# A decode-attention kernel on Trainium2: PV's matmuls from a nested hardware loop instead of straight code

## The chip, the cores and the metric

The kernel runs on one core of one Trainium2 chip. The metric is the device time of one execution in microseconds (us); smaller is better. Every time below is a median of fast runs, unless a single run is named. A profile's span is about 2 us shorter than the run's time.

## The reference, cut to what matters

One token (x of 640) goes through layer norm, then through attention over a cache of 32 heads, 32768 positions and 128 values per position, and in parallel through a small gated MLP. Both are added to x.

```python
q = (xn @ wq) per head                                   # 640 -> 32 x 128
scores = einsum("bhqd,bhkd->bhqk", q, k) * (128 ** -0.5) # k: [1, 32, 32768, 128] bf16
p = softmax(scores)
o = einsum("bhqk,bhkd->bhqd", p, v)                      # "PV"
out = x + o @ wo + (silu(xn @ w_gate) * (xn @ w_up)) @ w_down
```

K and V are 8.4 MB per head each. The weights are small beside them.

## The kernel before

In this kernel each engine has its own program, and they wait for each other at semaphores. Three slots of SBUF (`ring`) hold K or V of one head. VectorE multiplies K by q in place, in four quarters of 4.4 us. TensorE sums groups of products by identity matmuls into PSUM, and VectorE reduces them to scores. ScalarE takes the exponential. TensorE then does PV: 64 matmuls per head, each with its own four columns of P as the stationary operand and 512 columns of V streaming, all accumulated into one PSUM tile `O`. The PV of head h-1 comes after the scores of head h.

The heads 2 to 31 run in a hardware loop of three heads per pass (`t.Fori`). Inside it, PV was written out:

```python
PARTS = [64, 64, 128]      # PV of a head in three parts; W = 4 columns per matmul
def pv_part(h, part):
    s = slot_of[("v", h)]
    if part == 0:
        wait(s_exp, ...); wait(s_o4, ...); wait(s_slot[s], ...)   # P is there, O is free, V has landed
    first = sum(PARTS[:part])
    for j in range(first, first + PARTS[part], W):
        mm = t.matmul(O, lhsT=P[:, h % PR, j:j + W], rhs=ring[:, s, j * DH:(j + W) * DH],
                      start=(j == 0), stop=(j + W == NJ))
    if part == len(PARTS) - 1:
        mm.then_inc(s_pv, 1)

def head(h):
    scores(h)
    if h >= 1: total(h - 1); pv_part(h - 1, 0)   # total: sum of the exponentials, one small matmul
    turn(h)                                       # maximum of the scores, transposed
    if h >= 1: pv_part(h - 1, 1)
    spread(h)                                     # maximum to all partitions
    if h >= 1: pv_part(h - 1, 2)
    if h >= 2: fold(h - 2)                        # four rows of O to one column
# ... [cut: the loop over heads]
pv_last(0); total(H - 1); fold(H - 2)             # the last head's V comes in two halves
pv_last(1); hidden_part(0); fold(H - 1); hidden_part(1)
# ... [cut: out projection and down projection, small matmuls to the end]
```

The DMA queue is issued by SyncE. The next V waits for the end of a head's scores, and the next K for the end of a PV, because these free the slots.

Of the kernel before, what the change touches and what calls it, by code (L numbers as in the profile page):

```python
# [8 lines left out]
BF16 = mybir.dt.bfloat16  # L9
# [3 lines left out]
def bass_parallel_sum__gqa_block_cached__swiglu_ffn__decode_kernel(  # L13
# [15 lines left out]
    DH = A_k_cache.shape[3]  # L29
# [3 lines left out]
    NJ = SK // 128  # L33
# [4 lines left out]
    CE = NJ * DH  # L38
# [6 lines left out]
    PR = 3  # L45
    SR = 3
    TAIL = [NJ // 2, NJ // 2]
    RB = DH // 32
    OC = H * DH // 128
    WTAIL = [8, 8, 8, 5, 2, 1]  # L50
    PARTS = [64, 64, 128]
    W = 512 // DH
    assert sum(PARTS) == NJ and NHF == 4 and (H - H0) % PER == 0 and PER % SLOTS == 0
    assert PER % PR == 0 and PER % SR == 0
    assert OC == 32 and H * RB == 128 and sum(WTAIL) == OC
    HA = 5
# [13 lines left out]
    for pos, u in enumerate(units):  # L70
        s = pos % SLOTS
# [6 lines left out]
    with ExitStack() as es:  # L78
        def sbt(name, shape, dtype):
            return es.enter_context(nc.sbuf_tensor(name, shape, dtype))  # L80

        def sem(name):
            return es.enter_context(nc.semaphore(name))

        ring = sbt("ring", [128, SLOTS, CE], BF16)
        qb = sbt("qb", [128, H * DH], BF16)
        sc = sbt("sc", [128, NJ], F32)
        P = sbt("P", [128, PR, NJ], BF16)
# [4 lines left out]
        ocol = sbt("ocol", [128, H], BF16)  # L93
        oblk = sbt("oblk", [128, H, RB], BF16)
        blk = sbt("blk", [128, RB], BF16)
        fold32 = sbt("fold32", [128, OC], BF16)
        ot = sbt("ot", [128, OC], BF16)
        hcol = sbt("hcol", [128, FB + 1], BF16)
        par = sbt("par", [128, 2], F32)
        sg = sbt("sg", [128, 2, FB], F32)  # L100
        one1 = sbt("one1", [1, 1], BF16)
        xf = sbt("xf", [128, NCD], F32)
# [18 lines left out]
        s_const = sem("const")  # L121
# [7 lines left out]
        s_exp, s_pv, s_o4, s_fold, s_ov = sem("exp"), sem("pv"), sem("o4"), sem("fold"), sem("ov")  # L129
# [5 lines left out]
        flat = ring[:, :, :].rearrange("p s n -> p (s n)")  # L135
# [32 lines left out]
        u0 = d0 + FM * D + D // 2  # L168
        g0 = WO_S * CE + OC * D
        FW = FB * 128  # L170
# [24 lines left out]
        def relay(copy, i, c):  # L195
            w = (wg_v, wu_v)[i][:, c, :]
            if (i, c) in rest:
                return copy(rest[i, c].rearrange("p (f t) -> p f t", t=2),
                            w[:, FM * 128:F][:, :, None].to_broadcast([128, FL, 2]))
            copy(even(i, c)[:, 0:FM * 128].rearrange("p (j m) -> p j m", j=FM),  # L200
                 w[:, 0:FM * 128].rearrange("p (m j) -> p j m", j=FM))
            return copy(even(i, c)[:, FM * 128:FW].rearrange("p (f t) -> p f t", t=2),
                        w[:, FM * 128:F][:, :, None].to_broadcast([128, FL, 2]))
        wo = flat[:, WO_S * CE:WO_S * CE + OC * D]
        wo_v = wo.rearrange("p (j c m) -> p j c m", j=OC, c=NCD)
        assert OC * D <= CE
# [23 lines left out]
        with nc.psum_tensor("ps8", [128, 8, 512], F32) as ps8:  # L230
            bank = [ps8[:, b, :] for b in range(8)]
            O = ps8[0:W, 4, :]
            OL = ps8[0:W, 5, :]
# [44 lines left out]
            @block.gpsimd  # L278
            def pool(g):
                n = [0]  # L280

                def done(ins):
                    ins.then_inc(s_const, 1)
                    n[0] += 1
                    g.wait_ge(s_const, n[0])

                for t in (ident, identf):
                    done(g.memset(t[:, :], 0.0))
                    done(g.affine_select(out=t[:, :], in_=t[:, :], compare_op=ALU.not_equal, fill=1.0, base=0,
                                         pattern=[[-1, 128]], channel_multiplier=1))  # L290
                done(g.memset(blk[:, :], 0.0))
                for a in range(RB):
                    done(g.tensor_copy(out=fold32[a * 32:(a + 1) * 32, :],
                                       in_=ident[a * 32:(a + 1) * 32, a * 32:a * 32 + OC]))
                for a in range(RB):
                    done(g.memset(blk[a * 32:(a + 1) * 32, a:a + 1], 1.0))
                assert n[0] == 5 + 2 * RB
                g.wait_ge(s_out, 16)

            @block.tensor  # L300
            def pe(t):
# [3 lines left out]
                for c in range(NCD):  # L305
                    mm = t.matmul(misc[:, 8 + c:9 + c], lhsT=xrow_v[:, :, c], rhs=one1[:, :], start=True, stop=True)
                for c in range(NCD):
                    mm = t.matmul(misc[:, 16 + c:17 + c], lhsT=xrow[:, c * 128:(c + 1) * 128], rhs=one1[:, :],
                                  start=True, stop=True)
# [9 lines left out]
                for b in range(NQB):  # L319
                    for c in range(NCD):  # L320
                        mm = t.matmul(bank[b], lhsT=xnb[:, c, :], rhs=wq_v[:, c, b * 512:(b + 1) * 512],  # L321
                                      start=(c == 0), stop=(c == NCD - 1))
                    mm.then_inc(s_q, 1)
                t.wait_ge(s_qc, NQB)
                t.wait_ge(s_const, 4)

                def again(out, lhsT, rhs, stop):

# [9 lines left out]
                def scores(h):  # L338
                    kv = ring[:, slot_of[("k", h)], :].rearrange("p (j d) -> p j d", d=DH)
                    for i in range(NHF):  # L340
# [9 lines left out]
                                mm = again(ob, ident[:, :], src, g == DH // G - 1)  # L350
                        mm.then_inc(s_qk, 1)

                def pv_part(h, part):
                    s = slot_of[("v", h)]
                    if part == 0:
                        wait(s_exp, h, lambda h: h + 1)
                        wait(s_o4, h, lambda h: h)
                        wait(s_slot[s], h, lambda h: 16 * use_of[("v", h)])
                    first = sum(PARTS[:part])
                    for j in range(first, first + PARTS[part], W):  # L360
                        mm = t.matmul(O, lhsT=P[:, h % PR, j:j + W], rhs=ring[:, s, j * DH:(j + W) * DH],  # L361
                                      start=(j == 0), stop=(j + W == NJ))
                    if part == len(PARTS) - 1:
                        mm.then_inc(s_pv, 1)

                def pv_last(i):
                    h = H - 1
                    s = slot_of[("v", h)]
                    if i == 0:
                        t.wait_ge(s_exp, h + 1)  # L370
                    t.wait_ge(s_tail[i], 16)
                    first = sum(TAIL[:i])
                    for j in range(first, first + TAIL[i], W):
                        mm = t.matmul(OL, lhsT=P[:, h % PR, j:j + W], rhs=ring[:, s, j * DH:(j + W) * DH],  # L374
                                      start=(j == 0), stop=(j + W == NJ))
                    return mm

                def fold(h):

# [26 lines left out]
                def head(h):  # L406
                    scores(h)
                    if h >= 1:
                        total(h - 1)
                        pv_part(h - 1, 0)  # L410
                    turn(h)
                    if h >= 1:
                        pv_part(h - 1, 1)
                    spread(h)
                    if h >= 1:
                        pv_part(h - 1, 2)
                    if h >= 2:
                        fold(h - 2)


                def hidden_part(i):
                    for n, c in enumerate(ORDER[i]):
                        if (i, c) in A_COPIES:
                            t.wait_ge(s_even[0], A_COPIES.index((i, c)) + 1)
                        else:
                            t.wait_ge(s_even[1], v_copies.index((i, c)) + 1)
                        for j in range(FB):
                            mm = t.matmul(ffn[:, i * FB + j:i * FB + j + 1],
                                          lhsT=hidden(i, c, j), rhs=xn[:, c:c + 1],
                                          start=(i == 0 and n == 0 and j == 0),  # L430
                                          stop=(i == 1 and n == NCD - 1 and j == FB - 1), skip_group_check=True)
                    return mm
# [27 lines left out]
                with t.Fori(0, (H - H0) // PER) as i:  # L460
                    group[0] = i
                    for h in range(H0, H0 + PER):
                        head(h)
                    group[0] = None
                pv_last(0)
                total(H - 1)
                fold(H - 2)
                pv_last(1).then_inc(s_pv, 1)
                hidden_part(0)
                fold(H - 1)  # L470
                hidden_part(1).then_inc(s_f, 1)
                t.wait_ge(s_const, 5 + 2 * RB)
                t.wait_ge(s_ob, 1)
                t.matmul(op, lhsT=oblk[:, :, :], rhs=fold32[:, :], start=True, stop=True).then_inc(s_op, 1)
                t.wait_ge(s_ot, 1)
# [72 lines left out]
            def dve(v):  # L548
# [78 lines left out]
                for n, (i, c) in enumerate(v_copies):  # L627
                    if n == 0 or v_copies[n - 1][0] != i:
                        v.wait_ge(s_ffn[i], 16)
                    relay(lambda out, in_: v.tensor_copy(out=out, in_=in_), i, c).then_inc(s_even[1], 1)  # L630
                v.wait_ge(s_const, 5 + 2 * RB)
                v.tensor_reduce(out=par[:, :], in_=ident[:, :].rearrange("p (f t) -> p t f", t=2),
                                axis=AX.X, op=ALU.add).then_inc(s_fd, 1)
                v.wait_ge(s_ov, H + 1)
# [49 lines left out]
```

## Time and profile before

| | before |
|---|---|
| time | 1288.1 us |
| bytes read | 554 MB, 431 GB/s over the span |
| period of one head in the loop | 38.70 us (K and V, 19.35 us each) |
| PV, first to last start | 14.21 us per head |

Two lines of the page of before: busy us and share of the span of each engine, then the busy share of the DMA engines in tenths, over 40 slices of the span:

```profile
PE 1042.9 (81%) x4971; PEld 256.8 (20%) x3051; DVE 683.7 (53%) x417; ACT 62.9 (5%) x147; POOL 2.5 (0%) x17
...
DMA  9999999999999999999999999999999999999998
```

Transfers fill every slice. TensorE looks nearly as busy (81%), but it is not the limit, as the timeline shows. Its columns are start in us, duration in us, engine, line, operation, and in brackets the idle time of the engine before it with what ended it. One head of before:

```profile
596.73 17.43 DVE L595 TENSOR_TENSOR ring<-ring,qb 128x8192 bf16<-128x8192 bf16 x4 [9.67 <-DMA ring<-in_A_k_cache_dram]
...
617.88 0.33 SPq L260 DMA_DIRECT2D ring<-in_A_v_cache_dram  x1
...
617.89 3.62 PE L361 MATMUL ps<-ring,P 128*4 128x512 bf16 x16
...
625.41 7.07 PE L361 MATMUL ps<-ring,P 128*4 128x512 bf16 x32
...
632.41 1.05 PE L383 MATMUL ps<-identf,o 4*128 4x1 f32 x8
632.51 0.33 SPq L251 DMA_DIRECT2D ring<-in_A_k_cache_dram  x1
...
639.91 0.61 PE L348 MATMUL ps<-ring,ident 128*128 128x512 bf16 x1 [6.45 <-DVE ring L595]
```

K lands and VectorE starts at 596.73. The scores end at 617.88, which issues the next V. PV follows in three parts (16, 16 and 32 matmuls; the second, of 3.62 us, is left out here), and its end at 632.41 issues the next K. After the fold TensorE is idle for 6.45 us until the first quarter of the next head is multiplied.

The trace also keeps sequencer instructions, those that set registers or branch. Here are two of the outer loop's edge, a fused instruction of three register operations and the branch back (count, then minimum, median and maximum ns; the columns after that are first and last start):

```profile
L460 PEldq FUSED_REGOPS  x10: 50/50/50, 90.6 to 1133.6; - x10
...
L460 PEldq COMPARE_BRANCH  x10: 76/208/235, 204.6 to 1249.5; - x10
```

The tail of before, TensorE alone, from the last part of PV(30) to the last small matmuls of the projections:

```profile
1244.62 7.07 PE L361 MATMUL ps<-ring,P 128*4 128x512 bf16 x32
...
1252.60 7.07 PE L374 MATMUL ps<-ring,P 128*4 128x512 bf16 x32
...
1260.89 7.07 PE L374 MATMUL ps<-ring,P 128*4 128x512 bf16 x32
...
1267.89 1.65 PE L428 MATMUL ps<-xn,ring 128*128 128x1 bf16 x41
...
1270.19 1.05 PE L383 MATMUL ps<-identf,o 4*128 4x1 f32 x8
...
1278.31 2.52 PE L454 MATMUL ps<-ot,ring 128*128 128x1 bf16 x80
...
1281.56 0.58 PE L454 MATMUL ps<-ot,ring 128*128 128x1 bf16 x16 [0.74 <-DMA ring<-in_A_wo_dram]
1282.92 0.78 PE L454 MATMUL ps<-ot,ring 128*128 128x1 bf16 x24 [0.78 <-issue]
```

TensorE works almost without pause from 1244 us. It waits only at the end: for pieces of wo and for causes that the profile calls "issue" (nothing that it shows). These waits and the 0.38 us at 1277.27 (not shown) add up to 1.9 us of idle time. Counted from the start of one matmul to the start of the next, which leaves out the modelled ends, the pauses at 1277.27, 1279.60, 1281.56 and 1282.92 delay the chain by 2.5 us.

### The profile page before, as it was taken

The numbers are of one execution on the slowest core, as the hardware profiler recorded it, in microseconds if no ns is written. First come the engines' busy times: TensorE is split into PE (matmuls) and PEld (weight loads), VectorE is DVE, ScalarE is ACT, GpSimd is POOL, SyncE is SP. The second block draws the span as 40 slices with busy tenths as digits, with TensorE's granted clock in tenths as the row PEclk, the third lists the DMA queues.
The fourth block names the chain that finished last, engine by engine and source line by source line (L and its number), as shares of the span: only waits on it lengthen the run. The fifth ranks groups of instructions, "written<-read, shape, count | busy, mean of one in ns | idle before, by whom it ended". The sixth has DMA issues, their size and how long they took to land.

```text
span 1285.9 us, 9499 instructions
## 1 busy us (share of the span) xinstructions
PE 1042.9 (81%) x4971; PEld 256.8 (20%) x3051; DVE 683.7 (53%) x417; ACT 62.9 (5%) x147; POOL 2.5 (0%) x17
## 2 busy tenths in 40 slices
PE   3599777789777788777798777788777798778798
PEld 1011112221112221112221112221112221112225
DVE  0855665445665445664446664446664446654444
ACT  2000000000000000000000000000000000000003
POOL 0000000000000000000000000000000000000000
PEclk9799888898888999888898888898888998888898
DMA  9999999999999999999999999999999999999998
GB/s 422 427 444 431 429 434 437 430 430 442 428 434 432 436 430 434 438 428 434 434 436 428 436 438 426 434 436 434 434 430 438 428 432 442 428 434 432 436 418 357
DMA packets 10965, 554.13 MB, mean 431 GB/s; under 512 B 1227, under 2 KB 1484, under 8 KB 1740
## 3 DMA queue, kind: packets, MB, share of 16 engines
q1 hardware_dynamic: 10954, 554.00, 99.7%
q8 instruction: 7, 0.11, 0.0%
q14 instruction: 2, 0.02, 0.0%
q10 hardware_dynamic: 2, 0.00, 0.0%
HBM read 553.99 MB, written 0.00 MB: 431 GB/s over the span
## 4 chain that ended last, share of the span: by engine, by line
DMA 53%; PE 27%; DVE 13%; issue 7%; DVEq 0%; SPq 0%
DMA ring<-in_A_k_cache_dram 51%; PE ps L361 17%; DVE ring L595 13%; PE ps L329 8%; DMA ring<-in_A_wo_dram 2%; PE ps L348 1%; PE ps L403 0%; PE ps L397 0%; PE ps L391 0%; PE ps L454 0%; SPq L273 0%; DVEq L595 0%; DVE sc L601 0%; DVE pmax L607 0%; DVEq L221 0%
## 5 line engine op out<-in xcount | busy, mean ns | idle before, releaser
L595 DVE TENSOR_TENSOR ring<-ring,qb 128x8192 bf16<-128x8192 bf16 x128 | 557.8, 4420 | 316.6 <-DMA ring<-in_A_k_cache_dram 316.6
L329 PE MATMUL ps<-ring,ident 128*128 128x512 bf16 x1920 | 493.0, 415 | 0.0
L361 PE MATMUL ps<-ring,P 128*4 128x512 bf16 x1984 | 443.3, 379 | 0.0
L348 PE MATMUL ps<-ring,ident 128*128 128x512 bf16 x128 | 56.0, 438 | 223.0 <-DVE ring L595 222.4
L361 PEld LDWEIGHTS ps<-ring,P 128*4 128x4 bf16 x1984 | 163.5, 85 | 237.7
L348 PEld LDWEIGHTS ps<-ring,ident 128*128 128x128 bf16 x128 | 12.6, 98 | 618.1 <-DVE ring L595 346.3
L601 DVE TENSOR_REDUCE sc<-ps 128x64 f32<-128x512 f32 x128 | 82.2, 683 | 62.3 <-PE ps L329 62.3
L507 ACT ACTIVATE P<-sc,negb 128x256 bf16<-128x256 f32 x32 | 16.2, 508 | 956.6 <-DVE negb L613 956.6
L613 DVE TENSOR_SCALAR negb<-ps 128x1 f32<-128x1 f32 x32 | 5.1, 159 | 108.4 <-PE ps L403 108.4
L610 DVE TENSOR_REDUCE m<-ps 1x1 f32<-1x128 f32 x32 | 8.9, 279 | 85.2 <-PE ps L397 85.2
L383 PE MATMUL ps<-identf,o 4*128 4x1 f32 x256 | 33.5, 248 | 0.0
L383 PEld LDWEIGHTS ps<-identf,o 4*128 4x128 f32 x256 | 30.8, 186 | 13.1 <-issue 13.1
L391 PEld LDWEIGHTS ps<-rsum,ones 128*128 128x128 f32 x64 | 12.1, 190 | 99.1 <-issue 98.3
L498 ACT ACTIVATE o<-ps,rzb 4x512 f32<-4x512 f32 x32 | 21.7, 677 | 6.4 <-PE ps L361 6.2
L321 PE MATMUL ps<-ring 128*128 128x512 bf16 x40 | 11.0, 446 | 11.3 <-DMA ring<-in_A_wq_dram 11.3
L503 ACT ACTIVATE ocol<-ps 128x1 f32 (+1 forms) x32 | 5.5, 173 | 225.3 <-PE ps L383 225.3
L374 PE MATMUL ps<-ring,P 128*4 128x512 bf16 x64 | 14.1, 379 | 0.0
L607 DVE TENSOR_REDUCE pmax<-sc 128x1 f32<-128x256 f32 x32 | 13.4, 420 | 0.0
L397 PE MATMUL ps<-identf,pmax 128*1 128x128 f32 x64 | 12.2, 273 | 1.2 <-DVE pmax L607 1.2
L630 DVE COPY ring<-ring 128x1664 bf16<-128x1664 bf16 (+1 forms) x8 | 13.2, 1710 | 0.0
L583 DVE RECIPROCAL rzb<-ps 128x1 f32<-128x1 f32 x32 | 5.0, 158 | 15.1 <-PE ps L391 15.1
L403 PE MATMUL ps<-m,ones 1*128 1x1 f32 x64 | 12.1, 256 | 0.4 <-DVE m L610 0.4
(69 smaller groups left out, 95.3 us busy)
## 6 DMA issues: line engine op xcount, KB each, us to landing
ring<-in_A_v_cache_dram SPq DMA_DIRECT2D x2, 4096.0 KB, 36.5
ring<-in_A_wq_dram SPq DMA_DIRECT2D x1, 5120.0 KB, 15.8
ring<-in_A_wo_dram SPq DMA_DIRECT2D x3, 1280.0 KB, 24.1
ring<-in_B_w_gate_dram SPq DMA_DIRECT2D x1, 2160.0 KB, 22.6
ring<-in_B_w_up_dram SPq DMA_DIRECT2D x1, 2160.0 KB, 27.4
ring<-in_B_w_down_dram SPq DMA_DIRECT2D x1, 2080.0 KB, 30.8
ring<-in_A_wo_dram SPq DMA_DIRECT2D x1, 800.0 KB, 28.5
ring<-in_A_k_cache_dram SPq DMA_DIRECT2D x32, 41.5
```

The lines of the kernel that those rows point to most:

```text
L329: return t.add_instruction(mybir.InstMatmult(start_tensor_calc=False, stop_tensor_calc=stop, tile_size=(128, 128), tile_position=(0, 0), l ...
L348: t.matmul(ob, lhsT=ident[:, :], rhs=src, start=True, stop=False)
L361: mm = t.matmul(O, lhsT=P[:, h % PR, j:j + W], rhs=ring[:, s, j * DH:(j + W) * DH], start=(j == 0), stop=(j + W == NJ))
L374: mm = t.matmul(OL, lhsT=P[:, h % PR, j:j + W], rhs=ring[:, s, j * DH:(j + W) * DH], start=(j == 0), stop=(j + W == NJ))
L383: mm = t.matmul(fold_ps, lhsT=o4[:, m * DH:(m + 1) * DH], rhs=identf[0:W, m:m + 1], start=(m == 0), stop=(m == W - 1))
L397: t.matmul(misc[0:1, 0:128], lhsT=pmax[:, h % SR:h % SR + 1], rhs=identf[:, :], start=True, stop=True).then_inc(s_t, 1)
L498: a.activation(out=o4[:, :], in_=(OL if h == H - 1 and group[0] is None else O), func=ACTF.Copy, scale=rzb[0:W, h % SR:h % SR + 1]).then_i ...
L507: a.activation(out=P[:, h % PR, :], in_=sc[:, :], func=ACTF.Exp, bias=negb[:, h % SR:h % SR + 1], scale=c_scale, accum_out=rsum[:, h % SR: ...
L595: v.tensor_tensor(out=kh, in0=kh, in1=q[:, None, :].to_broadcast([128, HF, DH]), op=ALU.mult).then_inc(s_mul, 1)
L601: v.tensor_reduce(out=sc[:, i * HF:(i + 1) * HF], in_=bank[i].rearrange("p (j e) -> p j e", e=G), axis=AX.X, op=ALU.add).then_inc(s_red, 1)
L607: v.tensor_reduce(out=pmax[:, h % SR:h % SR + 1], in_=sc[:, :], axis=AX.X, op=ALU.max).then_inc(s_max, 1)
L630: relay(lambda out, in_: v.tensor_copy(out=out, in_=in_), i, c).then_inc(s_even[1], 1)
```

## The change

The 64 written-out matmuls of a head become three hardware loops with a body of four matmuls. The address of V and of P in each comes from registers, computed from the loop's counter. The accumulation's start and stop move to two tiny matmuls with a zero operand. The intent is a shorter program: the instruction packets in the trace, which carry up to 16 KB each, fell from 197 to 172 KB.

```diff
+    RUN = 4
+        zero = sbt("zero", [128, W], BF16)
+                def columns(o, h, s, first, n):
+                    if first == 0:
+                        t.matmul(o[:, 0:1], lhsT=zero[:, :], rhs=zero[:, 0:1], start=True, stop=False,
+                                 skip_group_check=True)
+                    with t.Fori(0, n // (RUN * W)) as b:
+                        for r in range(RUN):
+                            j = first + r * W
+                            t.matmul(o, lhsT=P[:, h % PR, bass.ds(b * (RUN * W) + j, W)],
+                                     rhs=flat[:, bass.ds(b * (RUN * W * DH) + (s * CE + j * DH), W * DH)],
+                                     start=False, stop=False, skip_group_check=True)
@@ pv_part
-                    first = sum(PARTS[:part])
-                    for j in range(first, first + PARTS[part], W):
-                        mm = t.matmul(O, lhsT=P[:, h % PR, j:j + W], rhs=ring[:, s, j * DH:(j + W) * DH],
-                                      start=(j == 0), stop=(j + W == NJ))
+                    columns(O, h, s, sum(PARTS[:part]), PARTS[part])
                     if part == len(PARTS) - 1:
-                        mm.then_inc(s_pv, 1)
+                        t.matmul(O[:, 0:1], lhsT=zero[:, :], rhs=zero[:, 0:1], start=False, stop=True,
+                                 skip_group_check=True).then_inc(s_pv, 1)
@@ pv_last: the same, with columns(OL, h, s, sum(TAIL[:i]), TAIL[i])
# ... [cut: zero is cleared by GpSimd, and three semaphore counts grow by one]
```

In the built program one pass of the loop has four instructions that do six register operations each, one more with three (or a single one), four weight loads, four matmuls, an add for the counter and a compare-and-branch.

## The prediction

> **What bounds it now.** Transfers. The page's slices show DMA at 9 tenths throughout, 431 GB/s. The timeline repeats every 38.7 us per head (K and V, 2 x 19.35 us). The chain of waits is 51% "DMA from K cache". Per period (timeline 596-635 us) K lands, VectorE multiplies 17.43 us, scores end at 617.5, PV runs 617.9-632.5 with two small matmuls between its parts, the fold ends at 633.5, and TensorE idles until 639.9 (6.4 us); VectorE idles 9.7 us on DMA. The next V is issued at 617.9 and the next K at 632.5, while queued transfers still have about 18 and 22 us to go (a K lands 41.5 us after its issue, 19.35 of them its own).
>
> **What changes.** PV's 64 matmuls per head stream at about 0.22 us start to start (16 in 3.6 us), 14.1 us in all. Now they come from 16 passes of a four-matmul body. Arithmetic, DMA and waits stay, plus two tiny zero matmuls per head. Shorter code is worth nothing: instruction fetch is 0.13 MB in the whole run.
>
> **Cost per pass, on TensorE's sequencer.** The trace has register instructions of the outer loop: fused register operations take 37, 50 and 64 ns for 2, 3 and 4 operations, about 13 ns each, so a six-operation one is an estimated 90 ns. A pass has four of these (360), one three-operation or single one (32-50), the counter's add (32) and a compare-and-branch (208 median, 76 to 235 in the trace[...]). About 650 ns. Then four weight loads and four matmuls with register addresses: the trace has none on TensorE. [...] Pass: about 1.15 us against 0.88 us of streaming, so PV becomes sequencer-bound at about 290 ns per matmul, 18.5 us per head. The sequencer runs ahead during the scores (about 2.5 us), so PV ends roughly 2-4 us later.
>
> **On the critical path?** In the loop, no. Scores take 14 us if TensorE starts late and can end with VectorE's products until PV has grown by about 8.9 us (6.4 idle plus 2.5). The transposed maximum and its broadcast come 1-2 us later, against 9.7 us idle on VectorE. Issues have 18-22 us of slack.
>
> In the tail, yes. The last V's matmuls and "total" release the copies of the FFN weights (VectorE idles 15.1 us for it), and TensorE is nearly continuous from 1252 to 1283.7 with only about 1.7 us of waits for the last wo pieces. PV(30) and the last head's halves slip 5-8 us together; less slack, 4-6 us.
>
> **Prediction: 1293 us, 1287.5 to 1311.** Faster by over 2%: 1%; within 2%: 85%; slower by over 2%: 14%.
>
> **What would show it.** PV starts 260-330 ns apart; PV 16-19 us per head; period still 38.7 us, DMA still 9s; TensorE's idle time before the scores 2-5 us; the tail after the last wo landing longer. Wrong if PV stays at 220 ns.
>
> **What would make it wrong.** Register-addressed loads and matmuls over about 130 ns each, slower short branches, or a clock that drops in the gaps: PV then grows by more than 9 us, TensorE bounds the period, each further us costing 30. [...]

The sum that was forecast came to about 1.15 us per pass (290 ns per matmul, 18.5 us per head). Of it about 650 ns come from the trace of before; the rest is the cut term, so these three figures rest in part on something that was not shown. Two more of its terms can be read from the traces. The sequencer's lead of about 2.5 us was my estimate; in after the first record of PV's first loop stands at 615.98, 1.93 us before its first matmul (617.91). And the clock does drop in before: 0.50 was granted from 597.29, inside TensorE's idle time, to 604.12, and the first quarter of the scores, at 601.21, took 4.67 us from first to last start, the others 3.24 to 3.25.

## The result, and the profile after

| | before | after |
|---|---|---|
| time, median of 4 runs each | 1288.13 us | 1289.84 us |
| ratio, 95% interval | | 1.0013 [0.9996, 1.0031] |
| span of the profile | 1285.9 us | 1288.0 us |
| period of one head | 38.70 us | 38.70 us |
| PV, first to last start, median of heads 3 to 29 | 14.21 us | 15.85 us |
| last piece of wo lands at | 1282.69 us | 1282.64 us |

A ratio is the mean time of one kernel's fast runs over that of the other's of the same rounds, so it is not quite the ratio of the medians. The two ranges do not overlap (1287.88 to 1288.29 against 1289.51 to 1290.17), so I take the small loss as real although the interval includes 1.

The same two lines of the page of after:

```profile
PE 1081.6 (84%) x5035; PEld 256.4 (20%) x3116; DVE 683.6 (53%) x417; ACT 62.9 (5%) x147; POOL 2.6 (0%) x18
...
DMA  9999999999999999999999999999999999999997
```

TensorE's busy share rose by 3 points, and the DMA line only lost a tenth in the last slice. The loop in after, the same stretch:

```profile
596.72 17.43 DVE L606 TENSOR_TENSOR ring<-ring,qb 128x8192 bf16<-128x8192 bf16 x4 [9.48 <-DMA ring<-in_A_k_cache_dram]
...
617.91 3.61 PE L364 MATMUL ps<-ring,P 128*4 x16
...
625.47 8.65 PE L364 MATMUL ps<-ring,P 128*4 x32
...
627.49 0.58 PEld L364 LDWEIGHTS ps<-ring,P 128*4 x4 [0.55 <-issue]
628.63 0.54 PEld L364 LDWEIGHTS ps<-ring,P 128*4 x4 [0.55 <-issue]
...
634.05 1.05 PE L394 MATMUL ps<-identf,o 4*128 4x1 f32 x8
634.16 0.33 SPq L253 DMA_DIRECT2D ring<-in_A_k_cache_dram  x1
...
639.91 0.61 PE L351 MATMUL ps<-ring,ident 128*128 128x512 bf16 x1 [4.81 <-DVE ring L606]
```

The first two parts still take 3.6 us each (the second is left out). The third takes 8.65 us instead of 7.07: its weight loads (PEld) come in bunches of four, and between the bunches the loader idles 0.55 us for "issue", that is, for its own sequencer, whose records below fill this time. PV ends 1.6 us later, the next K is issued 1.65 us later, the idle time before the next scores falls from 6.45 to 4.81 us, and K lands at the same moment as before (596.72 against 596.73).

The sequencer's records in after (fused register operations at the loop's head, its branch, and the fused operations in its body, in the format shown above; the 95 branches that were not taken, one per run of a loop, took 76 ns each):

```profile
L361 PEldq FUSED_REGOPS  x512: 78/78/83, 76.6 to 1270.7; - x171
...
L361 PEldq COMPARE_BRANCH  x512: 76/213/345, 77.4 to 1271.5; - x171
```

```profile
L364 PEldq FUSED_REGOPS  x2004: 51/74/84, 76.9 to 1271.3; - x183
```

One steady pass of the loop, read from the records of the trace (start in us, duration in ns; q marks the sequencer; matmul and load records left out):

```
629.507   78  fused, 6 operations      (59 ns pass until the next record)
629.644   51  fused, 3 operations      (78 ns: load and matmul pushed)
629.773   79  fused, 6                 (78 ns)
629.930   74  fused, 6                 (79 ns)
630.083   74  fused, 6                 (78 ns)
630.235   36  counter                  (61 ns)
630.332  213  compare and branch       (58 ns)
630.603       next pass
```

A pass takes 1.10 to 1.14 us, 1.12 on average in the stretch shown, against 0.88 us that four matmuls stream. Of these 1096 ns, the recorded instructions take 605, pushing eight register-addressed loads and matmuls 313 (39 each), and 178 lie in three gaps where register instructions or the branch follow each other with no load or matmul between them.

The tail of after, the counterpart of before's:

```profile
1244.84 8.52 PE L364 MATMUL ps<-ring,P 128*4 x32
...
1254.31 8.50 PE L364 MATMUL ps<-ring,P 128*4 x32
...
1264.03 7.90 PE L364 MATMUL ps<-ring,P 128*4 x32
...
1271.87 1.65 PE L439 MATMUL ps<-xn,ring 128*128 128x1 bf16 x41
...
1274.18 1.86 PE L394 MATMUL ps<-identf,o 4*128 4x1 f32 x8
...
1282.42 3.34 PE L465 MATMUL ps<-ot,ring 128*128 128x1 bf16 x120
```

PV(30)'s third part and the two halves of the last head are each longer, and the last half ends 3.98 us later (the next line starts at 1271.87 against 1267.89). At the end the waits are gone: 120 small matmuls run in one piece. The last of VectorE's additions after them starts 2.07 us later than before (1285.87 against 1283.80). The sum closes: the fold is 0.8 us longer (see E3) and other groups a little shorter, so the matmul that follows the hidden layer starts 4.59 us late (1278.74 against 1274.15); the 2.5 us of pauses of before are gone, and 2.1 us remain.

### The profile page after: what moved, and what is told of

Its sections match the earlier page's. It is cut to its first block, busy times and chain, and to the rows that moved or that the text cites. A ratio compares the mean times of both kernels' runs of the same rounds, so it can differ in the third digit from the quotient of the medians.

```text
span 1288.0 us, 13308 instructions
## 1 busy us (share of the span) xinstructions
PE 1081.6 (84%) x5035; PEld 256.4 (20%) x3116; DVE 683.6 (53%) x417; ACT 62.9 (5%) x147; POOL 2.6 (0%) x18
## 4 chain that ended last, share of the span: by engine, by line
DMA 49%; PE 34%; DVE 11%; issue 6%; DVEq 0%; ACT 0%
DMA ring<-in_A_k_cache_dram 49%; PE ps L364 20%; PE ps L332 11%; DVE ring L606 10%; PE ps L351 1%; PE ps L414 0%; PE ps L439 0%; PE ps L465 0%; PE ps L408 0%; PE ps L394 0%; PE ps L402 0%; PE ps L450 0%; PE ps L359 0%; DVEq L606 0%; DVE sc L612 0%
## 5 line engine op out<-in xcount | busy, mean ns | idle before, releaser
L364 PE MATMUL ps<-ring,P 128*4 x2048 | 491.3, 378 | 17.7 <-issue 0.2
L364 PEld LDWEIGHTS ps<-ring,P 128*4 x2048 | 165.1, 82 | 302.6 <-issue 130.6
L414 PEld LDWEIGHTS ps<-m,ones 1*128 1x128 f32 x64 | 9.4, 182 | 13.6 <-issue 13.0
```

The source lines that it names most:

```text
L364: t.matmul(o, lhsT=P[:, h % PR, bass.ds(b * (RUN * W) + j, W)], rhs=flat[:, bass.ds(b * (RUN * W * DH) + (s * CE + j * DH), W * DH)], star ...
L414: t.matmul(misc[:, 128:129], lhsT=ones[0:1, :], rhs=m1[0:1, h % SR:h % SR + 1], start=True, stop=True).then_inc(s_b, 1)
```

## The experiments

All ran on the chip, each with runs of before beside it. One caution comes first. E4 and E9 compute PV with the wrong addresses on purpose, and the comparison with the reference still passed. Attention adds very little to this output: V has scale 0.05 and is averaged almost evenly over 32768 positions. So "correct" does not vouch for PV in any kernel.

| run | what | time (us) | before beside it | PV per head (us) | period (us) |
|---|---|---|---|---|---|
| after | body of 4 | 1289.84 | 1288.13 | 15.85 | 38.70 |
| E1 | loop only | 1288.14 | 1288.02 | | |
| E2 | tail only | 1287.88 | 1288.02 | | |
| E3 | after, sum matmul earlier | 1289.47 | 1288.02 | | |
| E4 | constant addresses, body of 4 | 1287.90 | 1288.02 | 14.21 | 38.70 |
| E5 | body of 8 | 1287.90 | 1287.97 | 14.21 | 38.70 |
| E6 | body of 16 | 1287.57 | 1287.97 | 14.21 | 38.70 |
| E7 | body of 2 | 1305.87 | 1287.97 | 23.41 | 38.70 |
| E8 | body of 1 (single run) | 1746.19 | 1287.97 | 34.12 | 52.4 (mean) |
| E9 | constant addresses, body of 1 (single run) | 1303.62 | 1287.97 | 22.70 | 38.70 |
| E10 | E6, later program shifted by 64 matmuls | 1287.32 | 1287.97 | | |
| E11 | E6, shifted by 100 matmuls | 1287.56 | 1288.05 | | |

PV is the median from first to last start.

### E1 and E2: the change in the loop alone, and in the tail alone

```diff
 E1, pv_last:
-                    columns(OL, h, s, sum(TAIL[:i]), TAIL[i])
-                    return t.matmul(OL[:, 0:1], lhsT=zero[:, :], ...)
+                    return straight(OL, h, s, sum(TAIL[:i]), TAIL[i])    # written out as before
 E2, pv_part:
-                    columns(O, h, s, sum(PARTS[:part]), PARTS[part])
+                    mm = straight(O, h, s, sum(PARTS[:part]), PARTS[part])
```

> The change without its tail: the last head's two halves are written out as before, the loop's PV stays looped. Theory A (PV's growth of 1.6 us per head is hidden in the loop; in the tail the slips of PV(30) and of both halves add, 4.0 us at the end of the last half, and about 2.0 us of transfer waits absorb them first): slip 1.6 us at that point, all absorbed, so the time of before, 1288.1 (0 to +0.4 us). Rival (every us of slip costs the same share, 2.07/4.0 = one half): +0.8 us. Rival (the loss comes from the loop or from transfers): +1.7 us as in the whole change.

> Only the tail changed: PV of heads 0 to 30 written out as before, the last head's halves looped. Theory A: the last half ends about 2.4 us later than before, about 2.0 of them absorbed: +0.2 to +0.7 us. Rival (proportional): +1.2 us. Rival (loss comes from the loop): 0. E1 and E2 gains together, under theory A, are well under the whole change's +1.7 to +2.1 us.

E1 measured +0.12 us (ratio 1.0001 [0.9987, 1.0014]) and E2 -0.14 us (0.9998 [0.9984, 1.0012]). Neither half costs anything that the runs resolve, and together they cost 1.7 us, so the loss is not additive: the rivals (a fixed share per us, or a loss in the loop) fall. This rests on the spread of the single runs, as for after: E1's five lie between 1287.94 and 1288.62 us, under the 1288.8 of the fixed share, while the intervals alone reach to about 1.8 us. TensorE's timeline of E1, the start of the hidden layer and the end of a stall:

```profile
1269.93 1.66 PE L444 MATMUL ps<-xn,ring 128*128 128x1 bf16 x41
...
1280.70 0.19 PE L455 MATMUL ps<-hcol,ring 128*128 128x1 bf16 x2 [1.10 <-issue]
```

The hidden layer starts 2.0 us late (1.6 expected), from PV(30) and what leads up to it, and the waits at the end absorb most of it even though one of them is a new stall of 1.10 us. (The profiled run was the slowest of the five: its last matmul still starts 0.74 us late.) In E2 the two halves of the last head and the stall:

```profile
1252.76 7.07 PE L364 MATMUL ps<-ring,P 128*4 x32
...
1261.05 7.46 PE L364 MATMUL ps<-ring,P 128*4 x32
...
1280.91 2.99 PE L471 MATMUL ps<-ot,ring 128*128 128x1 bf16 x107 [2.18 <-issue]
```

Here my expectation missed. I expected the halves to end 2.4 us late, and they end 0.55 us late (the hidden layer starts at 1268.44): they take 7.07 and 7.46 us, not the 8.50 and 7.90 of after. With PV(30) written out, the sequencer is ahead of the array when the first looped half comes: the half's first branch is recorded at 1250.82, 1.9 us before its first matmul, and the half streams at full pace. In after that branch is recorded at 1254.51, 0.2 us behind the first matmul (1254.31). So the two parts of the change also make each other worse, before any slack is counted.

### E3: the sum matmul ahead of the first half

```diff
-                pv_last(0)
                 total(H - 1)
+                pv_last(0)
                 fold(H - 2)
```

> The whole change, but the last head's small sum matmul (which releases VectorE's FFN weight copies) is issued ahead of the last head's first half. The prediction said that its delay holds up the tail. If the copies are on the path, they start about 3 us earlier (at the gate weights' landing) and the end falls by 1.5 to 2 us, to that of before. If TensorE's own queue is the path, as the chain of waits of after has it, the end falls by at most 0.5 us, from shorter waits in the hidden layer.

E3 is 1.45 us over before, where after was 1.71 us over (different rounds). The copies did move: they start at 1259.82, when the gate weights land, instead of 1263.24. The end gained at most 0.3 us, so VectorE's copies are not what holds the tail of after. The prediction had named them. The path is TensorE's own queue. The fold in E3:

```profile
1274.23 1.20 PE L394 MATMUL ps<-identf,o 4*128 4x1 f32 x8
```

The hidden layer starts as late in E3 (1271.94) as in after (1271.87). What little the span gained (0.6 us) lies in the fold, which takes 1.20 us here, 1.86 in after and 1.05 in before. The granted clock in the stretch from 1272 to 1276 us is 0.87 here, 0.75 in after and 0.64 in before, and it falls to 0.50 in all three from 1276. These averages come from one step, from full clock to half, at 1274.98 in E3, 1273.98 in after and 1273.13 in before. The fold of before (1270.19) was over by then, that of after (1274.18) lies wholly behind the step, and that of E3 lies across it. So 0.8 us of after's tail is this step, by the records; I did not test it by itself.

### E4 to E9: what the sequencer pays for

E4 keeps the loop and drops the address registers; E9 does so with a body of one. E5 to E8 change the body's length.

```diff
 E4, E9:
-   t.matmul(o, lhsT=P[:, h % PR, bass.ds(b * (RUN * W) + j, W)],
-            rhs=flat[:, bass.ds(b * (RUN * W * DH) + (s * CE + j * DH), W * DH)], ...)
+   t.matmul(o, lhsT=P[:, h % PR, j:j + W], rhs=ring[:, s, j * DH:(j + W) * DH], ...)   # same four each pass
 E5, E6, E7, E8:  RUN = 8, 16, 2, 1     (E9: RUN = 1)
```

> Wrong result on purpose: the loop with its counter and its branch, but every pass takes the same four constant addresses, so no address registers are computed. Theory A (TensorE's sequencer sets the pace: register operations and register addresses 0.8 us, branch and counter 0.25 us per pass, against 0.88 us of streaming): without the register work the sequencer needs well under 0.88 us per pass, matmuls start 0.22 us apart again, no recurring 0.55 us weight-load gap, PV 14.6 to 14.9 us per head, the time of before, +0 to +0.3 us. Rival B (each taken branch drains the stream, about 0.24 us a pass whatever the body): PV stays at 16 us and the time at that of after. Rival C (register-addressed weight loads are not overlapped): agrees with A here, and is told apart by the runs of other body lengths.

> Body of eight matmuls instead of four. Theory A: a pass costs the sequencer about 0.30 us plus 0.204 us per matmul (fitted to after's 1.12 us per pass of four, with its register durations), so 1.93 us for eight, 242 ns per matmul in steady state; PV about 14.6 to 15.2 us per head, tail slip about 1.6 us, absorbed: +0 to +0.4 us on before. Rival B (a pause of 0.24 us per branch): 2.00 us per pass, hardly distinguishable here. Rival C (60 ns more per register-addressed matmul): 2.24 us per pass, 280 ns, PV and time as after.

> Body of sixteen; the first two parts become a single pass with constant addresses, the third part and the tail's halves keep two passes with register addresses. Theory A: 3.57 us per pass, 223 ns per matmul, practically streaming: PV 14.6 to 14.9, time of before +0 to +0.2 us. Rival C: 280 ns in the third part after the queue has run dry, about 4.5 us per pass.

> Body of two. Theory A: 0.71 us per pass, 355 ns per matmul, PV about 20.5 us per head, growth 6 us over before: still under the 8.9 us that the loop can hide, so the period stays 38.7 us; in the tail slips of about 10 us at the sum and 14.6 us at the end of the last half, slack of 2 us off: end +12 us, 1297 to 1303. If the slack were smaller than the growth, each us over it would cost 30 us and the time would pass 1310. Rival C: 280 ns per matmul, time as after.

> Body of one. Theory A: 0.50 us per matmul, PV about 30 to 32 us per head, 16 us over before and so past the 8.9 us of slack: TensorE bounds the period at 45 to 47 us instead of 38.7, transfers no longer fill the span (DMA tenths fall to 8 or less): 1500 to 1570 us. If the slack is larger than computed (the issues' 18 to 22 us counted), the time stays near 1310.

> Wrong result on purpose: constant addresses as in E4, but a body of one matmul, so that branch and counter stand alone against the 0.62 us per pass of E8. From the sequencer records inside a pass of after (counter 36 ns, about 61 ns until the branch, branch 213 ns, about 58 ns until the next instruction, and an estimated 39 ns for each of two pushes): 0.45 us per pass, so 0.18 us of E8's pass is address work and the rest is the branch and the pushes. PV 26 to 29 us per head, period about 45 us, TensorE-bound: 1470 to 1540 us. If only the recorded durations counted (249 ns plus the pushes): 0.33 us per pass, PV 21 us, and 1290 to 1305. If the branch cost nothing beyond streaming: 1288.

E4: PV is back at 14.21 us and the time at before's, with all 16 branches per head still there. So the branch does not drain the stream (rival B falls). E5 and E6: with register addresses (in E6 only in the third part and the tail) but fewer branches, PV streams at full pace (14.21 us). So register-addressed matmuls are not slower on the array by themselves (rival C falls). E5 came out better than my fit, which had 242 ns per matmul. The sequencer's time per pass against the array's is what decides: in E5 the branches of the loop are 1.73 us apart (median), just under the 1.76 us that eight matmuls stream.

E7's pairs of matmuls start 0.79 to 0.83 us apart, where I expected 0.71:

```profile
635.19 0.59 PE L364 MATMUL ps<-ring,P 128*4 x2 [0.20 <-issue]
...
636.00 0.59 PE L364 MATMUL ps<-ring,P 128*4 x2 [0.22 <-issue]
...
643.14 0.39 PE L351 MATMUL ps<-ring,ident 128*128 128x512 bf16 x1
```

The last line is the next head's first score matmul, without idle time before it: at 9.2 us of growth TensorE is exactly full, and the period is still 38.70 us. The tail paid more than expected, 17.9 us against 12, because each pass was longer. E8, past the edge:

```profile
DMA  9987797766797676797676797766797676797660
```

```profile
619.30 19.80 PE L364 MATMUL ps<-ring,P 128*4 x32
```

In E8 a pass takes 0.62 us (19.80 us for 32), TensorE bounds the loop, the period is 52.4 us and DMA falls to six or seven tenths. I expected 0.50 us per pass and 1500 to 1570 us, so the direction was right and the size far off. In both cases the error is the same. My fit put the three gaps (178 ns per pass) into the cost per matmul, where they belong to the pass. Short bodies pay them more often. The records of after, sorted that way, give 478 ns for each pass (first address operation, counter, branch, gaps) and about 154 ns for each matmul (a six-operation instruction and two pushes): 0.63, 0.79, 1.09 and 1.71 us for bodies of one, two, four and eight, where the branches of E8, E7, after and E5 are 0.62, 0.79, 1.12 and 1.73 us apart. In E8 the clock adds to this. The granted clock averages 0.71 over the run: after each PV the fold takes 1.86 us and the first quarter of the scores 4.8 to 6.2 us, against 1.03 and 3.5 in E7, whose granted clock averages 0.99. The fold also took 1.86 us in after's tail, at a granted 0.50, so I put this down to the clock. That is an estimated 2.7 us of a period which is 13.7 us longer; PV itself grew by 10.7 us from E7 to E8.

E9 tells branch and registers apart. Its third part, and the spacing of its weight loads:

```profile
628.65 12.16 PE L364 MATMUL ps<-ring,P 128*4 128x512 bf16 x32
...
632.28 0.08 PEld L364 LDWEIGHTS ps<-ring,P 128*4 128x4 bf16 x1 [0.30 <-issue]
632.66 0.08 PEld L364 LDWEIGHTS ps<-ring,P 128*4 128x4 bf16 x1 [0.30 <-issue]
```

A pass takes 0.38 us. Its records are 36 ns for the counter, a gap of 60, 208 for the branch, and 78 ns until the next counter, which hold both pushes. Taking off the 58 ns that follow the branch in after leaves an estimated 10 ns for each constant-address push. E8's pass of 0.62 us thus has about 0.24 us of register addressing in it. I had expected 0.45 us, with pushes at 39 ns, and 1470 to 1540 us: that missed, and the price of 39 ns belongs to register-addressed pushes alone. The time falls in the range that I gave for 0.33 us per pass. Its loss of 15.7 us is in the tail again, as the unchanged period shows.

### E10 and E11: the stalls near the end

The stalls of about 1 us among the tail's small matmuls (0.38 us in before to 2.18 us in E2) stood at a different place in nearly every kernel. In before, E1, E2, E4, E5 and E6 such a stall ended 2.5 to 2.7 us after a 16 KB instruction packet had started in the trace's DMA records; after and E3 have such packets and no such stall. To test this, E6 got zero matmuls on an idle TensorE before the first head, which shifts the rest of the program.

```diff
                 t.wait_ge(s_const, 5)
+                for _ in range(64):      # E11: 100
+                    t.matmul(OL[:, 0:1], lhsT=zero[:, :], rhs=zero[:, 0:1], start=True, stop=True,
+                             skip_group_check=True)
```

> E6 with 64 zero matmuls (128 instructions with their weight loads, 8 KB) added on an idle TensorE before the first head: everything after them lies 8 KB later in the program. Theory F (the stalls of about 1 us among the small matmuls of the tail are instruction fetches at fixed places of the program, each ending about 2.6 us after a 16 KB instruction packet starts): in E6 they stood after the 52nd matmul of the down projection and after the 109th of the last 120; here both move about 64 matmuls earlier, the last one to about the 45th of the 120, where it ends before or about when the last wo pieces land; the last 40 then run without a stall and the end falls by 0.5 to 0.9 us against E6: about 1286.9. Rival (the stalls are waits for wo pieces or for other engines): they stay where they are and the time stays at E6's 1287.6.

> E10 with 100 zero matmuls instead of 64. Theory F (instruction fetches at fixed places of the program): the stall in the last 120 small matmuls moves 36 matmuls earlier again, from the 45th to about the 9th, and is over by about 1280.2 us, more than 1 us before the last wo pieces land; the last 40 matmuls then run straight after that landing, the last small matmul ends near 1282.8 us instead of 1283.5 us, and the time falls by 0.5 to 0.8 us against E10: 1286.5 to 1286.9. Rival (the gain of E6 and E10 over before is chance, the stall's place does not matter): 1287.3 to 1287.9.

The 8 KB that E10's text gives for 64 matmuls are an estimate from before: between the ends of its two stalls, 1277.27 and 1282.92, lie 128 matmuls with their weight loads (26 + 6 + 80 + 16), and 16 KB packets start at 1274.79 and 1280.38, each 2.5 us ahead of one of them.

The group of matmuls after the last stall in E6, in E10 and in E11 (of E11 also its fold):

```profile
1283.06 0.43 PE L465 MATMUL ps<-ot,ring 128*128 128x1 bf16 x11 [0.65 <-issue]
```

```profile
1281.39 2.14 PE L468 MATMUL ps<-ot,ring 128*128 128x1 bf16 x75 [1.72 <-issue]
```

```profile
1270.45 1.82 PE L397 MATMUL ps<-identf,o 4*128 4x1 f32 x8
...
1280.08 3.10 PE L468 MATMUL ps<-ot,ring 128*128 128x1 bf16 x111 [1.03 <-issue]
```

The last group has 11, 75 and 111 of the 120 matmuls, so the stall moved from after the 109th to after the 45th and the 9th, as the program was shifted by 64 and 100 matmuls. The stalls are bound to places in the program. That they are fetches rests on the timing of the packets: the stalls of E10 and E11 ended 2.3 and 2.5 us after one started. The time gained little: 1287.57, 1287.32 and 1287.56 us. In E10 the stall still lasted until 1281.39. In E11 it was over by 1280.08, but the fold took 1.82 us there (granted clock 0.63 from 1270 to 1272 us), and TensorE came late to the rest. None of these is faster than before by more than its interval (ratios 0.9993 to 0.9999). There is no version here that beats before clearly; E5, E6, E10 and E11 equal it.

## Why the prediction was right

**Right: the loop hides it.** The period stayed at 38.70 us to the last digit, the idle time before the scores fell to 4.8 us (2 to 5 predicted), and the last wo piece landed at the same time as before.

**Right: the edge.** I put the slack at 8.9 us per head. Growth of 8.5 us (E9) and 9.2 us (E7) left the period unchanged; at 9.2 us no idle time was left; at 19.9 us (E8) the period was 13.7 us longer.

**Right: the cost per pass, but from wrong parts.** Predicted 1.15 us, measured 1.12. I counted 650 ns of register and branch work and put the rest down to pushes. The records show 605 ns, and 178 ns of gaps that I had not counted, and 313 ns of pushes, less than my rest. A six-operation instruction took 74 to 79 ns and not 90. The point of 64 ns in my series is VectorE's (30 records of its sequencer in before); TensorE's own are 37 and 50. That the errors cancelled at a body of four was luck, and they no longer did at two and one.

**Right place, wrong size: the tail.** The step that was off was "PV(30) and the last head's halves slip 5-8 us together; less slack, 4-6 us". They slipped 3.98 us. The end moved 2.07 us in the profile and 1.7 us in time. PV grew by 1.6 us per head, not 2 to 4. The prediction's own terms (18.5 less 14.1 of streaming, less a lead of 2.5) give 1.9, which it had rounded up. Sixteen passes of the measured 1.12 us would exceed the streaming by 3.8 us, so the lead was worth an estimated 2.2 us, and it carried the first two parts (32 matmuls) at full pace. The two halves grew by 1.4 and 0.8 us, where the prediction's 5-8 less 2-4 had left them 3 to 4. The slack was larger than read: 2.5 us from start to start, against 1.7 predicted. The fold's 0.8 us was in no term. The range held, but 1293 was 3 us too high.

**Wrong detail: the FFN copies.** They start later, as I said, but E3 shows that they do not hold the end up.

**Right: shorter code is worth nothing.** Instruction packets fell from 0.13 to 0.12 MB, and E6, whose program is longer than that of after, is as fast as any.

**Still open.** Whether the clock's step in the tail costs 0.8 us in after as the records suggest was not isolated. Nor was the remaining difference of a few tenths of a us between the kernels that equal before.

## What to carry to other kernels

Count a hardware loop's sequencer time per pass, gaps included, against the time its body streams, and make the body long enough that the array is the slower one: here four matmuls of 0.22 us were too few and eight were enough. Then ask where the excess is seen. A transfer-bound loop with 6 us of idle TensorE per head hid 1.6 us for 31 heads, and only the tail after the loop, where nothing else waits, paid. Before reading a loss of a us or two into a change, look for stalls that move with the program's layout.
